# An adaLN block in one kernel: a new share-out of the first norm between ScalarE and VectorE, and a new order of the q phase's columns and of VectorE's list

## The chip, the cores and the metric

The kernel is one launch on one core of one Trainium2 chip. The metric is device time in microseconds; lower is better. The engines go by the names of the profile: PE is TensorE, DVE is VectorE, ACT is ScalarE, POOL is GpSimd, and SP is SyncE, whose queue issues nearly all DMAs.

## The reference, cut to what matters

```python
mod = (silu(c) @ w_mod)                       # 6 vectors of 1024: sa, ca, ga, sb, cb, gb
h = layernorm(x) * (1 + ca) + sa              # x is [2048, 1024], bfloat16
x = x + ga * linear_attention(h, wqkv, wo)    # phi(q), phi(k); phi(t) = t + 1 if t > 0 else exp(t)
h = layernorm(x) * (1 + cb) + sb
x = x + gb * ((silu(h @ w_gate) * (h @ w_up)) @ w_down)
```

Only the first line of h and the q and k products of the attention are touched by the change in earnest. The mean and the variance of the first norm are those of each row of x; the modulation vectors ca and sa come out of a product of the small vector silu(c) with w_mod.

## The kernel before

**Tiles and stages.** The 2048 rows are 16 tiles of 128 rows, in four chunks of four tiles. XRES holds the rows. HT holds, in two buffers (chunk number modulo 2), a chunk's normalised rows turned round: eight slices (dt 0 to 7) of 128 features by 512 rows. The order of the program is: first norm of chunk 0; q phase of chunk 0; k phase of chunk 0; then for each of chunks 1 to 3 eight k groups and eight q groups; then the products that form the attention's output, and the feed-forward part. A group is eight matmuls of 512 columns into one PSUM bank.

**What sets the order.** Every engine runs its own list strictly in the order in which the program text issues it. A helper class records each operation, finds which earlier operations it depends on by the memory it touches (for PSUM by whole banks), and puts in semaphore waits. All operations are recorded through one helper, so every row of the profile has the line L176, and rows are told apart by their tiles. Side work is hung on the groups: `qside`, `kside`, `s1`, `s2`, `s3` are lists of closures that are issued after the group of that number.

**First norm of chunk 0.** The four tiles land at 3.62, 4.24, 5.80 and 6.58 us. Statistics are made in one of two ways: on VectorE (`ln1_stats_ops`: two half-tile bn_stats and an aggregate) or on ScalarE (`act_stats`: one Identity pass and one Square pass with accumulated sums, whose bulk output goes to a junk tile; `act_var` on VectorE then makes the negated variance). In the kernel before, ScalarE sums tile 1 and VectorE does tiles 0, 2 and 3; ScalarE normalises tiles 0 and 1 and VectorE tiles 2 and 3. GpSimd raises the variance to the power -0.5. TensorE turns each tile with eight transposes into PSUM (`tile_transposes`), and fills its waits with matmuls on zeros (`warm`). `mod_sc` makes columns of the modulation on TensorE (one-column matmuls into bank 0), `fin_ca` and `fin_sa` read them out on VectorE. `h0_first` scales a turned slice out of PSUM into HT, `raw_copy` copies two slices without scaling.

**q phase of chunk 0** (`q_phase_chunk0`). The first seven column groups of q go slice by slice, so that the work can begin before all weights and all modulation columns are there; `q_part` is one step of one group. In between stand the `mod_sc` columns, and `bias_mm`, which carries the shift sa through the q weights to a bias column (`BIASQ`), so that the first use of HT needs the scale alone. The eighth group comes last, into bank 0. `h0_shift` then adds the shift to HT for the k phase. `q_phi` evaluates phi: ScalarE writes exp and relu of the bank into four rotating buffers E1 and RL (`phi_evac`), and after each second group VectorE combines them (`phi_flush`). The norm of chunk 1's tiles (4 to 7) is woven into this list, and `th_dma` turns each of these tiles with an x-bar DMA transpose on SP's queue into the other buffer of HT.

**k phase of chunk 0 and chunk 1.** A k group's exp goes to E1 as well, and VectorE's flush reads the PSUM bank itself and so releases it. After the second k group `kside` holds `th_mod(1, dt)`, the eight modulations of chunk 1's slices; after the fourth and fifth it holds ScalarE's passes over tiles 10 and 11. Eight banks rotate; a k group of chunk 1 needs the bank of the k group of the same number of chunk 0.

```python
def th_mod(ch, dt):
    buf = ch % 2
    if dt % 2 == 0 or ch == 1:
        P.dve("tensor_scalar", out=HT[:, buf, dt, :], ...
    else:
        P.act("activation", out=HT[:, buf, dt, :], ...

for dt in range(NDT):
    add(kside, 1, lambda dt=dt: th_mod(1, dt))
for jj, k in ((0, 3), (1, 4)):
    add(kside, k, lambda jj=jj: act_stats(10 + jj))
```

Of the kernel before, what the change touches and what calls it, by code (L numbers as in the profile page):

```python
# [8 lines left out]
ACT = mybir.ActivationFunctionType  # L9
# [253 lines left out]
def bass_adaLN_cond__linear_attn_block__swiglu_ffn__prompt_kernel(  # L263
# [17 lines left out]
    NDT = D // 128  # L281
# [4 lines left out]
    with ExitStack() as es:  # L286
# [114 lines left out]
        def ca_load(p):  # L401
            P.dma("wca%d" % p, WCA[:, :, 512 * p:512 * p + 512], wmv[:, :, D + 512 * p:D + 512 * p + 512])

        def sa_load(p):
            P.dma("wsa%d" % p, WSA[:, :, 512 * p:512 * p + 512], wmv[:, :, 512 * p:512 * p + 512])

        def wq_load(i, n=1):
            P.dma("wq%d" % i, WQK[:, i:i + n, 0:D], wqkvv[:, i:i + n, 0:D])
# [6 lines left out]
        sa_load(1)  # L415
        wq_load(6)
        wq_load(7)
        sa_load(0)
        for j in range(2):
            P.dma("x1_%d" % j, XRES[:, 4 + j, :], xv[:, 4 + j, :])  # L420
        for i in (1, 0):
# [70 lines left out]

        def th_mod(ch, dt):
            buf = ch % 2
            if dt % 2 == 0 or ch == 1:
                P.dve("tensor_scalar", out=HT[:, buf, dt, :], in0=HT[:, buf, dt, :], scalar1=MODCOL[:, 0, dt:dt + 1],
                      scalar2=MODCOL[:, 1, dt:dt + 1], op0=ALU.mult, op1=ALU.add)
            else:
                P.act("activation", out=HT[:, buf, dt, :], in_=HT[:, buf, dt, :], func=ACT.Identity,
                      scale=MODCOL[:, 0, dt:dt + 1], bias=MODCOL[:, 1, dt:dt + 1])  # L500

        mod_first = [True]

        def mod_sc(w, c0, ms):
            for m in ms:
                for kt in range(NDT):
                    P.pe("matmul", out=PS[:, 0, c0 + m:c0 + m + 1], lhsT=w[:, kt, m * 128:(m + 1) * 128],
                         rhs=SILUC[:, kt:kt + 1], start=mod_first[0], stop=(kt == NDT - 1), skip_group_check=True)
                    mod_first[0] = False
# [61 lines left out]

        JUNK1 = T("junk1", 204 * KB, [128, 2, 512], BF16)

        def act_stats(st, c0=0, mid=None):
            n = (D - c0) // 512
            junk0 = HT[:, 1, 0:2, :] if st < 8 else JUNK1
            for fn_, sc_, acc_ in ((ACT.Identity, 1.0 / D, SUMX), (ACT.Square, D ** -0.5, SUMSQ)):
                P.act("activation", out=junk0[:, 0:n, :], in_=XRES[:, st, c0:D].rearrange("p (a b) -> p a b", a=n),
                      func=fn_, scale=sc_, accum_out=acc_[:, st:st + 1])
                if mid is not None:  # L580
                    mid()
                    mid = None

        def act_mv_ops(st):
            return [
# [7 lines left out]
                  op1=ALU.add)  # L593
            P.pool("tensor_tensor", out=RSTD[:, st:st + 1], in0=VE[:, st:st + 1], in1=NEGHALF[:, 0:1], op=ALU.pow)

        s0_, s2_, s3_ = ln1_stats_ops(0), ln1_stats_ops(2), ln1_stats_ops(3)

        def act_var(st):
            P.dve("scalar_tensor_tensor", out=MV[:, st, 1:2], in0=SUMX[:, st:st + 1], scalar=SUMX[:, st:st + 1],
                  in1=SUMSQ[:, st:st + 1], op0=ALU.mult, op1=ALU.subtract)  # L600
            P.dve("tensor_scalar", out=VE[:, st:st + 1], in0=MV[:, st, 1:2], scalar1=-1.0, scalar2=EPS, op0=ALU.mult,
                  op1=ALU.add)

        def act_xn(st, mean):
            P.dve("tensor_scalar", out=NMR[:, st:st + 1], in0=mean, scalar1=RSTD[:, st:st + 1],
                  scalar2=-1.0, op0=ALU.mult, op1=ALU.mult)
            P.act("activation", out=XRES[:, st, :], in_=XRES[:, st, :],
                  func=ACT.Identity, scale=RSTD[:, st:st + 1], bias=NMR[:, st:st + 1])

        def tile_transposes(*js):  # L610
            for dt in range(NDT):
                for j in js:
                    c = (dt % 2) * 512 + j * 128
                    P.pe("transpose", out=PSB[:, 4 + dt // 2, c:c + 128], in_=XRES[:, j, dt * 128:(dt + 1) * 128],
                         identity=IDENT[:])

        warm(13, bank=3)
        act_stats(1)
        for f in s0_:
            f()  # L620
        ln1_rstd1(0)
        s2_[0]()
        s2_[1]()
        act_xn(0, MV[:, 0, 0:1])
        tile_transposes(0)
        warm(5, bank=3)
        act_var(1)
        P.pool("tensor_tensor", out=RSTD[:, 1:2], in0=VE[:, 1:2], in1=NEGHALF[:, 0:1], op=ALU.pow)
        P.pool("tensor_scalar", out=NMR[:, 1:2], in0=SUMX[:, 1:2], scalar1=RSTD[:, 1:2], scalar2=-1.0,
               op0=ALU.mult, op1=ALU.mult)  # L630
        P.act("activation", out=XRES[:, 1, :], in_=XRES[:, 1, :], func=ACT.Identity, scale=RSTD[:, 1:2],
              bias=NMR[:, 1:2])
        s2_[2]()
        ln1_rstd1(2)
        s3_[0]()
        s3_[1]()
        s3_[2]()
        ln1_rstd1(3)
        ln1_xn(2)
        mod_sc(WCA, 8, range(2))  # L640
        tile_transposes(1, 2)
        ln1_xn(3)
        fin_ca(0, 2)
        tile_transposes(3)
        mod_sc(WCA, 8, range(2, 4))
        h0_first(0, "dve")
        h0_first(1, "dve")
        raw_copy(4, "dve")
        raw_copy(6, "act")
# [94 lines left out]

        def q_phase_chunk0(side):
            qb = [1, 2, 3, 4, 6, 7, 5]
            fin_ca(2, 2)
            for dt in (2, 3):
                h0_first(dt, "dve")
            for nts, dts in ((range(4), (0,)), (range(4), (1,)), ((4, 5, 6), (0, 1))):  # L750
                for nt in nts:
                    q_part(nt, qb[nt], dts)
            for nt in range(7):
                if nt == 3:
                    mod_sc(WCA, 8, range(4, 8))
                    fin_ca(4, 4)
                    for dt in (4, 5):
                        h0_scale_only(dt)
                q_part(nt, qb[nt], (2, 3))
            act_stats(4)  # L760
            for nt in range(7):
                if nt == 4:
                    mod_sc(WSA, 0, range(6, 8))
                    fin_sa(6, 2)
                    for dt in (6, 7):
                        h0_scale(dt)
                q_part(nt, qb[nt], (4, 5))
            mod_sc(WSA, 0, range(4, 6))
            fin_sa(4, 2, True)
            for nt in range(7):  # L770
                if nt == 2:
                    bias_mm((4, 5))
                q_part(nt, qb[nt], (6,))
            for nt in range(7):
                if nt == 1:
                    mod_sc(WSA, 0, range(4))
                    fin_sa(0, 4, True)
                    ln_ops[1][0]()
                    ln_ops[1][1]()
                if nt == 4:  # L780
                    bias_mm(range(4))
                    bias_fin()
                q_part(nt, qb[nt], (7,))
            ln_ops[1][2]()
            ln1_rstd1(5)
            for f in act_mv_ops(4):
                f()
            neg_rstd(4)
            q_phi = lambda nt: phi_evac(qb[nt] if nt < 7 else 0, PQT[:, nt, 0:512], bias=BIASQ[:, nt:nt + 1])
            for i, dt in enumerate((4, 5, 0, 1, 2, 3, 6, 7)):  # L790
                P.pe("matmul", out=PS[:, 0, :], lhsT=WQK[:, dt, 896:1024], rhs=HT[:, 0, dt, :], start=(i == 0),
                     stop=(i == 7))
            for dt in (4, 5):
                h0_shift(dt)
            ln1_xn(5)
            th_dma(5)
            for dt in range(4):
                h0_shift(dt)
            ln1_xn(4)
            th_dma(4)  # L800
            for nt in range(8):
                q_phi(nt)
                for f in side.get(nt, []):
                    f()
            qk_ctr[0] = 0

        def add(d, k, f):
            d.setdefault(k, []).append(f)
# [1 line left out]
        qside, kside = {}, {}  # L810
        ln_ops = [ln1_stats_ops(4 + jj) for jj in range(4)]

        def ln_x1(jj):
            for f in ln_ops[jj]:
                f()
            ln1_rstd1(4 + jj)
        for f in ln_ops[2]:
            add(qside, 1, f)
        for f in ln_ops[3]:
            add(qside, 1, f)  # L820
        add(qside, 1, lambda: ln1_rstd2(6))
        for jj in range(2, 4):
            add(qside, 3, lambda jj=jj: ln1_xn(4 + jj))
            add(qside, 3, lambda jj=jj: th_dma(4 + jj))
        for dt in range(NDT):
            add(kside, 1, lambda dt=dt: th_mod(1, dt))
        for jj, k in ((0, 3), (1, 4)):
# [252 lines left out]
        for st in range(NST):  # L1080
            for (sw, nh) in (((0, 0), (1, 0)), ((0, 1), (1, 1)))[st] if st < 2 else ((st, 0), (st, 1)):
                wo_part(sw, nh, range(4, 8) if st < 2 else range(8))
                done = wo_res(sw, nh)
            if st < 4:
                P.wait_for("sp", [done])
                if st < 3:
                    ch = st + 1
                    P.dma("xr%d" % (3 + ch), XRES[:, 4 * ch:4 * ch + 4, :], xv[:, 4 * ch:4 * ch + 4, :])
                else:
                    P.dma("stgx2", STGX[1][:], wmv[:, :, 5120:6144])  # L1090
            if st >= 1:
                ln2_sq(st - 1)
            for kt in ((), (0,), (1,), (2, 3), (4,), (5,), (6, 7))[st] if st < 7 else ():
                macc(STGX[0], kt)
            if st == 6:
                macc_split()
            if st == 8:
                mod_red()
                mod_fin_col(3, False)
            if st == 7:  # L1100
                for jj in range(4):
                    ln2_xn(jj)
                th2_dma()
            if st == 8:
                th2_mod()
            if st == 7:
                for q in range(4):
                    gu_load(q)
# [106 lines left out]
```

## Time and profile before

| What | Value |
|---|---|
| median of the timed runs | 829.2 us (3 runs, 828.35 to 829.22) |
| span of the profiled execution, first to last instruction | 827.0 us |
| PE busy | 817.0 us |
| DVE busy, of these in 30 to 40 us | 310.8 us, 9.90 of 10 |
| ACT busy, of these in 30 to 40 us | 197.3 us, 9.11 of 10 |
| first scaled q matmul on record | 12.71 us |
| landing of the columns 512 to 1023 of sa | 21.36 us |

The profile is that of one execution. The page gives no time of that execution beyond its span; the timed runs lie 1.35 to 2.2 us above it. A row of a timeline has the start and the length in us, the engine, the line (always L176 here), the operation, what it writes and reads, the count, and in brackets the idle time before it and what ended it. Some matmul records are missing, one in about fifty: a step between two matmuls that is exactly twice the usual one is a lost record and no wait.

### The profile page before, as it was taken

To read this page: it belongs to the slowest core of one execution; us is meant where nothing else is said; L and a number is where in the kernel's file an instruction comes from. 1 tells how busy PE (TensorE), PEld (TensorE's weight loads), DVE (VectorE), ACT (ScalarE), POOL (GpSimd) and SP (SyncE) were. 2 spreads that over 40 slices of the span, in tenths; PEclk is the share of its full clock that TensorE was granted. 3 is DMA by queue.
4 is the path that set the end of the run, shared out by engine and by line. 5 is a ranking of instruction groups with operands and counts; after the bars stand their busy time and mean duration, and the time that the engine had idled before them with its cause. 6 is when DMAs were issued, how large, how long until landed. Compare 5 with 4: busy or idle time off the path is not lost.

```text
span 827.0 us, 10428 instructions
## 1 busy us (share of the span) xinstructions
PE 817.0 (99%) x4244; PEld 376.1 (45%) x4323; DVE 310.8 (38%) x664; ACT 197.3 (24%) x336; POOL 40.7 (5%) x59
## 2 busy tenths in 40 slices
PE   8999999999999999999999999999999999999998
PEld 4544444444444444444444444444444444444444
DVE  5798988476945521111221112122111211221111
ACT  4658643123241111011111101111110111111011
POOL 1010000000130000030000003000000300000000
PEclk9999999999999999999999999999999999999999
DMA  9969665856697995700455570045557004553000
GB/s 317 283 151 225 156 169 144 185 166 200 164 256 234 289 256 153 175 27 23 133 149 152 154 177 29 20 128 153 152 153 185 26 19 124 153 153 87 0 26 26
DMA packets 199360, 119.32 MB, mean 144 GB/s; under 512 B 57992, under 2 KB 183056, under 8 KB 199312
## 3 DMA queue, kind: packets, MB, share of 16 engines
q1 hardware_dynamic: 199296, 118.65, 53.7%
q8 instruction: 34, 0.56, 0.3%
q14 instruction: 14, 0.11, 0.0%
q10 hardware_dynamic: 16, 0.00, 0.0%
HBM read 100.67 MB, written 4.33 MB: 127 GB/s over the span
## 4 chain that ended last, share of the span: by engine, by line
PE 95%; DMA 2%; DVE 1%; SPq 1%; issue 1%; ACT 0%; DVEq 0%; ACTq 0%
PE ps L176 95%; DMA wsa<-in_w_mod_dram 2%; DVE acc L176 1%; SPq L176 1%; DVE pkt L176 0%; DVE e L176 0%; DVE pqt L176 0%; ACT e L176 0%; DVE xres L176 0%; DVE ht L176 0%; DVEq L247 0%; ACTq L247 0%
## 5 line engine op out<-in xcount | busy, mean ns | idle before, releaser
L176 PE MATMUL ps<-h2t,gug 128*128 128x512 bf16 x878 | 210.1, 379 | 0.9
L176 PE MATMUL ps<-h2t,guu 128*128 128x512 bf16 x878 | 209.9, 379 | 0.9
L176 DVE TENSOR_TENSOR at<-sg,ps 128x512 bf16<-128x512 bf16 x112 | 77.0, 688 | 282.7 <-PE ps L176 270.5
L176 ACT ACTIVATE sg<-ps 128x512 bf16<-128x512 f32 x112 | 66.9, 597 | 309.7 <-PE ps L176 298.3
L176 PEld LDWEIGHTS ps<-h2t,guu 128*128 128x128 bf16 x896 | 87.7, 98 | 105.7
L176 PEld LDWEIGHTS ps<-h2t,gug 128*128 128x128 bf16 x896 | 87.6, 98 | 105.5
L176 PE MATMUL ps<-wd_a,at 128*128 128x512 bf16 (+1 forms) x502 | 111.9, 377 | 0.5
L176 PE MATMUL ps<-ht,wqk 128*128 128x512 bf16 x499 | 110.5, 379 | 1.0 <-issue 0.2
L176 PE MATMUL ps<-wd_b,at 128*128 128x512 bf16 (+1 forms) x377 | 84.7, 377 | 0.4
L176 PEld LDWEIGHTS ps<-wd_a,at 128*128 128x128 bf16 x512 | 50.1, 98 | 59.7
L176 DVE TENSOR_TENSOR ut<-att,gb_b 128x512 bf16<-128x512 bf16 (+1 forms) x32 | 13.9, 435 | 167.2 <-ACT att L176 167.2
L176 PEld LDWEIGHTS ps<-ht,wqk 128*128 128x128 bf16 x512 | 49.4, 98 | 59.0 <-DVE ht L176 0.7
L176 ACT ACTIVATE att<-ps 128x512 bf16<-128x512 f32 (+1 forms) x32 | 17.4, 591 | 182.1 <-PE ps L176 182.1
L176 PEld LDWEIGHTS ps<-wd_b,at 128*128 128x128 bf16 x384 | 37.5, 98 | 44.7
L176 PE MATMUL ps<-pk,xres 128*128 128x512 bf16 x250 | 55.4, 379 | 0.6 <-issue 0.5
L176 PE MATMUL ps<-mw,pqt 128*128 128x512 bf16 x249 | 55.5, 379 | 0.5 <-issue 0.2
L176 POOL TENSOR_SCALAR h2t<-h2t,modcol 128x512 bf16<-128x512 bf16 x32 | 26.3, 837 | 383.4 <-DMA h2t<-xn 383.4
L176 ACT ACTIVATE e<-ps 128x512 bf16<-128x512 f32 x56 | 33.2, 604 | 31.9 <-PE ps L176 20.2
L176 PEld LDWEIGHTS ps<-mw,pqt 128*128 128x128 bf16 x256 | 24.7, 98 | 30.2 <-issue 0.5
L176 PEld LDWEIGHTS ps<-pk,xres 128*128 128x128 bf16 x256 | 24.7, 98 | 29.9 <-issue 0.9
L176 ACT ACTIVATE junk<-xres 128x1024 bf16<-128x1024 bf16 x24 | 25.4, 1058 | 34.5 <-DVE xres L176 34.2
L176 DVE SCALAR_TENSOR_TENSOR xres<-ps,xres 128x512 bf16<-128x512 f32 x32 | 21.4, 688 | 11.8 <-PE ps L176 11.6
(107 smaller groups left out, 337.9 us busy)
## 6 DMA issues: line engine op xcount, KB each, us to landing
gug<-in_B_w_gate_dram SPq DMA_DIRECT2D x56, 512.0 KB, 4.0
guu<-in_B_w_up_dram SPq DMA_DIRECT2D x56, 512.0 KB, 5.3
xres<-in_A_x_dram SPq DMA_DIRECT2D x20, 256.0 KB, 4.4
rb<-recip_den SPq DMA_DIRECT2D x8, 512.0 KB, 11.5
stgx<-in_w_mod_dram SPq DMA_DIRECT2D x2, 2048.0 KB, 9.7
wd_a<-in_B_w_down_dram SPq DMA_DIRECT2D x4, 1024.0 KB, 7.4
out_dram<-xres SPq DMA_DIRECT2D x31, 128.0 KB, 1.7
xres<-in_A_x_dram SPq DMA_DIRECT2D x3, 1024.0 KB, 7.1
```

The costliest lines, as they stand in the source:

```text
L176: return getattr(e, method)(**kw)
```

## The change

The change has these parts.

- First norm: ScalarE sums tiles 0 and 2, VectorE makes the statistics of tiles 1 and 3. Tile 1 is normalised on VectorE and turned first, then tile 0 (normalised on ScalarE, behind the sums of tile 2), tile 3 and tile 2 (both normalised on VectorE). Five filler matmuls become three. The first four columns of ca are made as one and three, not as two and two; the second `fin_ca` moves from the q phase to a place between `h0_first(0)` and `h0_first(1)`.
- The load of the columns 0 to 511 of sa is split into two halves over kt. The q phase makes the four columns of sa in two parts, one for each half. Other column groups and the two bias products are moved by one to two q steps.
- ScalarE's Identity pass over tile 4 stays in the q phase; its Square pass moves behind `q_phi(1)`. Its junk output goes to JUNK1.
- VectorE's list from the end of the q phase: shifts of slices 4 and 5 first, then the second half of tile 5's statistics, then shifts of 0 to 3, then tile 5. Tile 6's statistics go behind `q_phi(0)`; tile 4's variance, tile 7's statistics, and tile 4's normalising with its transpose go behind `q_phi(1)`; tiles 6 and 7 are normalised and turned behind `q_phi(2)` and no longer behind `q_phi(3)`.
- For chunk 1 `th_mod` puts slices 0, 1 and 2 on ScalarE and 3 to 7 on VectorE.
- In the second norm, `mod_red`, `mod_fin_col(3, False)` and `th2_mod` move from st 8 to st 9.

```diff
-        def sa_load(p):
-            P.dma("wsa%d" % p, WSA[:, :, 512 * p:512 * p + 512], wmv[:, :, 512 * p:512 * p + 512])
+        def sa_load(p, k0=0, k1=8):
+            P.dma("wsa%d_%d" % (p, k0), WSA[:, k0:k1, 512 * p:512 * p + 512], wmv[:, k0:k1, 512 * p:512 * p + 512])
...
-            if dt % 2 == 0 or ch == 1:
+            if dt % 2 == 0 if ch != 1 else dt > 2:
...
         warm(13, bank=3)
-        act_stats(1)
-        for f in s0_:
+        act_stats(0)
+        for f in s1_:
             f()
-        ln1_rstd1(0)
-        s2_[0]()
-        s2_[1]()
-        act_xn(0, MV[:, 0, 0:1])
-        tile_transposes(0)
-        warm(5, bank=3)
-        act_var(1)
...
+        ln1_rstd1(1)
+        act_var(0)
+        pool_pow(0)
+        P.pool("tensor_scalar", out=NMR[:, 0:1], in0=SUMX[:, 0:1], scalar1=RSTD[:, 0:1], scalar2=-1.0,
                op0=ALU.mult, op1=ALU.mult)
...
+        act_stats(2)
         s3_[0]()
+        ln1_xn(1)
         s3_[1]()
         s3_[2]()
         ln1_rstd1(3)
-        ln1_xn(2)
-        mod_sc(WCA, 8, range(2))
-        tile_transposes(1, 2)
+        P.act("activation", out=XRES[:, 0, :], in_=XRES[:, 0, :], func=ACT.Identity, scale=RSTD[:, 0:1],
+              bias=NMR[:, 0:1])
+        act_var(2)
+        pool_pow(2)
+        tile_transposes(1)
+        warm(3, bank=3)
         ln1_xn(3)
-        fin_ca(0, 2)
+        tile_transposes(0)
+        mod_sc(WCA, 8, range(1))
         tile_transposes(3)
-        mod_sc(WCA, 8, range(2, 4))
+        ln1_xn_sum(2)
+        fin_ca(0, 1)
+        tile_transposes(2)
+        mod_sc(WCA, 8, range(1, 4))
         h0_first(0, "dve")
+        fin_ca(1, 3)
         h0_first(1, "dve")
...
             for nt in range(7):
-                if nt == 3:
+                if nt == 4:
                     mod_sc(WCA, 8, range(4, 8))
...
-            act_stats(4)
+            act_stats(4, (0,))
             for nt in range(7):
-                if nt == 4:
+                if nt == 6:
                     mod_sc(WSA, 0, range(6, 8))
...
-                if nt == 2:
+                if nt == 3:
                     bias_mm((4, 5))
...
                 if nt == 1:
-                    mod_sc(WSA, 0, range(4))
+                    mod_sc(WSA, 0, range(4), range(4))
+                if nt == 4:
+                    mod_sc(WSA, 0, range(4), range(4, 8))
                     fin_sa(0, 4, True)
                     ln_ops[1][0]()
-                    ln_ops[1][1]()
-                if nt == 4:
+                if nt == 6:
                     bias_mm(range(4))
                     bias_fin()
                 q_part(nt, qb[nt], (7,))
-            ln_ops[1][2]()
-            ln1_rstd1(5)
-            for f in act_mv_ops(4):
-                f()
-            neg_rstd(4)
...
             for dt in (4, 5):
                 h0_shift(dt)
+            ln_ops[1][1]()
+            ln_ops[1][2]()
+            ln1_rstd1(5)
+            for dt in range(4):
+                h0_shift(dt)
             ln1_xn(5)
             th_dma(5)
-            for dt in range(4):
-                h0_shift(dt)
-            ln1_xn(4)
-            th_dma(4)
...
         for f in ln_ops[2]:
-            add(qside, 1, f)
+            add(qside, 0, f)
+        add(qside, 1, lambda: act_stats(4, (1,)))
+        add(qside, 1, lambda: act_var(4))
+        add(qside, 1, lambda: pool_pow(4))
         for f in ln_ops[3]:
             add(qside, 1, f)
         add(qside, 1, lambda: ln1_rstd2(6))
+        add(qside, 1, lambda: ln1_xn_sum(4))
+        add(qside, 1, lambda: th_dma(4))
         for jj in range(2, 4):
-            add(qside, 3, lambda jj=jj: ln1_xn(4 + jj))
-            add(qside, 3, lambda jj=jj: th_dma(4 + jj))
+            add(qside, 2, lambda jj=jj: ln1_xn(4 + jj))
+            add(qside, 2, lambda jj=jj: th_dma(4 + jj))
...
-            if st == 8:
+            if st == 9:
                 mod_red()
                 mod_fin_col(3, False)
```

`pool_pow(st)` is the power on GpSimd as a helper of its own, and `ln1_xn_sum(st)` normalises a tile on VectorE with ScalarE's sum as the mean.

More of the change, by code (lines that the diff above doesn't have):

```diff
@@ L417, in bass_adaLN_cond__linear_attn_block__swiglu_ffn__prompt_kernel @@
         wq_load(7)
-        sa_load(0)
+        sa_load(0, 0, 4)
+        sa_load(0, 4, 8)
         for j in range(2):
@@ L502, in bass_adaLN_cond__linear_attn_block__swiglu_ffn__prompt_kernel, with mod_sc @@
         mod_first = [True]
-        def mod_sc(w, c0, ms):
+        def mod_sc(w, c0, ms, kts=range(NDT)):
             for m in ms:
-                for kt in range(NDT):
+                for kt in kts:
                     P.pe("matmul", out=PS[:, 0, c0 + m:c0 + m + 1], lhsT=w[:, kt, m * 128:(m + 1) * 128],
@@ L572, in bass_adaLN_cond__linear_attn_block__swiglu_ffn__prompt_kernel, with act_stats @@
         JUNK1 = T("junk1", 204 * KB, [128, 2, 512], BF16)
[L574 to L578, printed above, removed]
+        def act_stats(st, passes=(0, 1)):
+            junk0 = HT[:, 1, 0:2, :] if st < 4 else JUNK1[:]
+            for i in passes:
+                fn_, sc_, acc_ = ((ACT.Identity, 1.0 / D, SUMX), (ACT.Square, D ** -0.5, SUMSQ))[i]
+                P.act("activation", out=junk0, in_=XRES[:, st, :].rearrange("p (a b) -> p a b", a=2),
                       func=fn_, scale=sc_, accum_out=acc_[:, st:st + 1])
-                if mid is not None:
-                    mid()
-                    mid = None
         def act_mv_ops(st):
@@ L594, in neg_rstd @@
             P.pool("tensor_tensor", out=RSTD[:, st:st + 1], in0=VE[:, st:st + 1], in1=NEGHALF[:, 0:1], op=ALU.pow)
-        s0_, s2_, s3_ = ln1_stats_ops(0), ln1_stats_ops(2), ln1_stats_ops(3)
+        s1_, s3_ = ln1_stats_ops(1), ln1_stats_ops(3)
         def act_var(st):
@@ L602, in act_var @@
                   op1=ALU.add)
[L604 to L608, printed above, removed]
         def tile_transposes(*js):
@@ L615, in tile_transposes, with ln1_xn_sum, pool_pow @@
                          identity=IDENT[:])
+        def ln1_xn_sum(st):
+            P.dve("tensor_scalar", out=XRES[:, st, :], in0=XRES[:, st, :],
+                  scalar1=SUMX[:, st:st + 1], scalar2=RSTD[:, st:st + 1], op0=ALU.subtract, op1=ALU.mult)
+        def pool_pow(st):
+            P.pool("tensor_tensor", out=RSTD[:, st:st + 1], in0=VE[:, st:st + 1], in1=NEGHALF[:, 0:1], op=ALU.pow)
         warm(13, bank=3)
-        act_stats(1)
-        for f in s0_:
-            f()
-        ln1_rstd1(0)
-        s2_[0]()
-        s2_[1]()
-        act_xn(0, MV[:, 0, 0:1])
-        tile_transposes(0)
-        warm(5, bank=3)
-        act_var(1)
-        P.pool("tensor_tensor", out=RSTD[:, 1:2], in0=VE[:, 1:2], in1=NEGHALF[:, 0:1], op=ALU.pow)
-        P.pool("tensor_scalar", out=NMR[:, 1:2], in0=SUMX[:, 1:2], scalar1=RSTD[:, 1:2], scalar2=-1.0,
+        act_stats(0)
+        for f in s1_:
+            f()
+        ln1_rstd1(1)
+        act_var(0)
+        pool_pow(0)
+        P.pool("tensor_scalar", out=NMR[:, 0:1], in0=SUMX[:, 0:1], scalar1=RSTD[:, 0:1], scalar2=-1.0,
                op0=ALU.mult, op1=ALU.mult)
[L631 to L634, printed above, removed]
+        act_stats(2)
         s3_[0]()
+        ln1_xn(1)
         s3_[1]()
@@ L746, in q_phase_chunk0 @@
             qb = [1, 2, 3, 4, 6, 7, 5]
-            fin_ca(2, 2)
             for dt in (2, 3):
@@ L811, in bass_adaLN_cond__linear_attn_block__swiglu_ffn__prompt_kernel @@
         ln_ops = [ln1_stats_ops(4 + jj) for jj in range(4)]
[L813 to L816, printed above, removed]
         for f in ln_ops[2]:
-            add(qside, 1, f)
+            add(qside, 0, f)
+        add(qside, 1, lambda: act_stats(4, (1,)))
+        add(qside, 1, lambda: act_var(4))
+        add(qside, 1, lambda: pool_pow(4))
         for f in ln_ops[3]:
@@ L1103, in bass_adaLN_cond__linear_attn_block__swiglu_ffn__prompt_kernel @@
                 th2_dma()
-            if st == 8:
+            if st == 9:
                 th2_mod()
```

## The prediction

> **What bounds the kernel.** I read the page first.
>
> ```profile
> PE 817.0 (99%) x4244; PEld 376.1 (45%) x4323; DVE 310.8 (38%) x664; ACT 197.3 (24%) x336; POOL 40.7 (5%) x59
> ```
>
> TensorE is busy 817.0 of 827.0 us, so a change pays only where TensorE idles or does filler, and any new wait of TensorE goes straight to the end. The next view is TensorE's timeline of the first 45 us (start, length).
>
> ```profile
> 2.61 5.73 PE L176 MATMUL ps<-e,ident 128*128 128x512 bf16 x13 [0.24 <-DVE e L176]
> 8.64 0.62 PE L176 MATMUL ps<-ident,xres 128*128 128x128 bf16 x8 [0.31 <-ACT xres L176]
> 9.10 1.24 PE L176 MATMUL ps<-e,ident 128*128 128x512 bf16 x5
> ...
> 21.41 0.55 PE L176 MATMUL ps<-siluc,wsa 128*128 128x1 bf16 x16 [0.18 <-DMA wsa<-in_w_mod_dram]
> ...
> 28.04 17.21 PE L176 MATMUL ps<-ht,wqk 128*128 128x512 bf16 x77
> ```
>
> Filler (13 and 5 warm matmuls) fills the wait for the first norm. Useful matmuls of 512 columns follow each other by 0.216 us, turns (128 columns) by 0.056, column products by 0.025. From 28.04 on there is one unbroken row: 77 matmuls with 0.1 us of wait. So before 28 us less than 1.5 us can be won. After it there is only something to lose, and what could lose it stands in VectorE's timeline (27 to 47 us), then in ScalarE's (35 to 62 us):
>
> ```profile
> 36.80 0.99 DVE L176 TENSOR_SCALAR xres<-xres,mv,rstd 128x1024 bf16<-128x1024 bf16 x2
> ...
> 43.10 2.67 DVE L176 TENSOR_SCALAR ht<-ht,modcol 128x512 bf16<-128x512 bf16 x8 [1.54 <-DMA ht<-xres]
> ```
>
> ```profile
> 36.58 0.69 ACT L176 ACTIVATE e<-ps,biasq 128x512 bf16<-128x512 f32 x1 [0.89 <-DVE pqt L176]
> ...
> 38.87 2.07 ACT L176 ACTIVATE e<-ps 128x512 bf16<-128x512 f32 x4
> ...
> 59.33 1.21 ACT L176 ACTIVATE e<-ps 128x512 bf16<-128x512 f32 x2 [3.77 <-DVE pkt L176]
> ```
>
> Chunk 1's modulation (eight on VectorE, 0.324 apart) starts as the last x-bar transpose lands (42.98) and ends at 45.78; TensorE needs the last slice at 45.74. While VectorE waits 1.54 us, ScalarE goes on: four exps, then the sums of tiles 10 and 11.
>
> **First norm.** ScalarE gains two passes (2.33 us a tile, 4.27 to 6.60) and loses one normalising (1.24); VectorE loses a tile's statistics (1.29 + 0.21) and gains one normalising (0.54); GpSimd keeps four powers and a shift. By these rows: tile 1 lands 4.24, statistics to 5.98 (1.72 as for tile 0 now), power to 6.70, normalised 7.75. Tile 0 is summed 3.65 to 5.98, but on ScalarE tile 2's sums (6.01 to 8.34) stand ahead of its normalising: 9.55, against 8.59 now. Tile 3: power 9.48, normalised 10.06 (now 10.91). Tile 2: power queued behind tile 3's; the row where a power lay beside a normalising is 0.78 against 0.56, so 10.2, normalised 10.80. TensorE: filler to 8.13, tile 1's turns to 8.58, three fillers to 9.23, wait, tile 0's turns 9.6 to 10.05, eight columns, tile 3's to 10.7, tile 2's 10.86 to 11.3, 24 columns to 11.9. The first scaling out of PSUM ends 11.73, but the second waits for fin_ca(1, 3) behind those columns: 12.33 to 12.81. So q's second slice starts at 12.95, now 13.36: **0.4 won**.
>
> **Columns up to 28 us.** Same matmuls and columns. Gone: the wait for wsa (0.34 with a lost record taken out) because two more matmul pairs stand ahead, and 0.12 of small waits. New: 0.10 for slice 6, 0.07 and 0.23 around the bias, whose copy had three matmuls (0.65) as cover and now one (0.22). Splitting the wsa load adds one issue (0.43) on SP, hidden behind an x issue that sat 4.58 us on a full ring. The eighth group starts at 28.18, now 28.69: **0.5 won**, 0.45 left after a small wait for the shifts.
>
> **VectorE's list, 28 to 38 us.** It now runs without idle time. New: it waits 0.5 us until TensorE has read slice 4 (28.56) before it may shift it, and 0.4 us for the power of tiles 6 and 7 (0.70, row at 35.87). Added up by rows: shifts 0.53, tile 5's second half 1.02, shifts 1.05, normalising 0.46, tile 6 1.43, flush of phi 0/1 1.07, tile 4's variance 0.32, tile 7 1.62, normalising 0.46, then tiles 6 and 7: 38.0, now 37.8. The flush of 2/3 has slipped behind that, and with four buffers ScalarE's exp 6 waits for it: 38.8 instead of 36.58. The exps of k groups 0 and 1 come at 41.1 and 41.6 (now 38.87, 39.35).
>
> **SP.** Tile 4's transpose was issued at 32.9; its input is now ready at 36.7, so three transposes of 1.33 us queue: 36.7, 38.05, 39.4. From issue to landing the transposes at 56 to 64 us took 3.3, this one now 4.3: landing 42.7 or 43.7. Ends: 41.9 (ScalarE is not free before 42.0, however early they land) and 43.8. I take 43.0, nearer the 3.3, since the ring is emptier.
>
> **Chunk 1.** ScalarE takes slices 0 to 2, and everything behind them on its queue waits for the landing too. The view of the tile ht (count, then ns: least, median, most) has the price of one slice on each engine:
>
> ```profile
> L176 DVE TENSOR_SCALAR ht<-ht,modcol x16: 401/406/414, 43.1 to 97.8; 128x512 bf16<-128x512 bf16 x16
> ...
> L176 ACT ACTIVATE ht<-ht,modcol x8: 804/814/827, 65.1 to 97.4; 128x512 bf16<-128x512 bf16 x8
> ```
>
> ScalarE's take 0.81, 0.705 apart (70.66 to 71.36). Start 43.12, third slice 45.34, where TensorE, 0.45 early, wants it at 44.2: **+1.08**. Behind them: exps of k groups 2 to 7 and four passes. Exp 2 starts 45.24, exp 3 45.71; from there to exp 5's end the row is 6.04 (40.30 to 46.34): 51.7. VectorE frees the bank 0.9 later, 52.6; k group 4 of chunk 1 wants it at 51.87: **+0.79**. VectorE then begins tile 8's statistics at 54.8 instead of 50.57; from there 8.7 to the release of bank 3 (59.28): 63.4, wanted at 63.0: **+0.45**. ScalarE's next exp waits for the same (the 3.77 above), 63.45 for 59.33, and from there to 76 it has no slack (15.58 busy in 59.3 to 75.4), so chunk 2's last slice, 72.18 now, comes at 76.3. Chunk 2 starts 73.83 and wants it at 75.34: **+1.02**. Afterwards ScalarE waits 1.13 of every 1.73 us for TensorE and VectorE 1.07 at 83.2: the lag is gone, and the loss stays. The move of mod_red by one tile takes away a 0.06 wait at 227; the last use of H2T's modulation (POOL, done 234.6, then 3 later) is at 244, so that is hidden.
>
> Sum: -0.45 + 1.08 + 0.79 + 0.45 + 1.02 = **+2.9**, on a span of 827.0; the timed runs (median 829.2) lie 2.2 above the span, which I leave: 832.1.
>
> **Two rules weighed.** Modulation on ScalarE costs 0.705 a slice by the rows above, on VectorE 0.324. The Trainium skill, Perfetto Trace Analysis, Optimizing Scalar/DVE Operations, says moving work to ScalarE may pay when VectorE is saturated. By it VectorE's list would shorten by three slices, 0.97, and the sum for that step would be a gain instead of +1.08; I go by the rows, as VectorE sits idle just before and ScalarE's queue does not.
>
> The fillers follow each other by 0.427 until 8.1 and later matmuls by 0.216. The skill's TensorE: Matmul & The Clock Gate, Part 1, has the clock at half rate until a free-running window of about 3.4 us was busy. Tile 1's turns come 0.5 us earlier than any turn now; by it they and three fillers could be at half rate, 1.0 more, of which 0.37 lies in the wait for tile 0. No row here shows a turn at half rate; the first one, 0.3 us after the fillers, ran at 0.056, and the sum goes by that.
>
> **Rivals.** (1) The chain as summed: the price moves one for one with ScalarE's start, start - 40.2; with starts of 42.0 to 43.9, +1.9 to +3.7. Chance 0.60. (2) Only the first two waits count, as banks and buffers downstream have more slack than I read: -0.45 + 1.08 + 0.8, or less: +0.6 to +1.5. For it: each later wait is a small difference of long sums. 0.17. (3) Not slower: VectorE's list and the transposes get through early, ScalarE starts slices 0 to 2 by 40.2, and no wait is new; the 0.5 from the front stays: 828.7. It decides at 40.2. For it: the stalls of packets at 34.1 to 36.8 and 40.0 to 41.5 may go. Against: three issues of 1.33 from 36.7. 0.11. (4) Worse: a transpose stalls again (1.5 us at 40.0 to 41.5) and the new turns run at 0.107: +4 to +5. 0.10. What I have not seen: 0.02.
>
> Range 829.6 to 833.9: it leaves out (3), the end of (4) and the unseen, some 0.16. A difference of 0.2% (1.66 us) is about what measuring can tell from none. Faster by more: 0.02, the unseen. Within: (2) and (3), 0.28. Slower: (1) and (4), 0.70.
>
> **What would show it.** q's second slice at 12.9; the eighth group at 28.2; tile 7's normalising ending at 38.0; last transpose landing near 43; three ScalarE modulations 0.705 apart with idle time of ScalarE before them; TensorE waits at 44 to 46, 52, 63 and 74 to 76. Wrong if ScalarE starts them by 40, or if TensorE's row from 44 to 76 stays unbroken.

## The result and the profile after

The changed kernel takes 831.64 us (median of 5 runs, 831.08 to 832.9), the kernel before on the same chip 828.7 (5 runs, 828.27 to 829.22): ratio 1.004, 95% interval 1.0029 to 1.0051, so 2.9 us slower. The profiled span is 829.8 against 827.0. One execution of an experiment, e1's profiled one, took 1238.73 us where the other ten of that kernel took 829.23 to 830.91; it counts in nothing below.

Of the page, the row of busy times and the chain, by engine, come first.

```profile
PE 817.5 (99%) x4242; PEld 375.7 (45%) x4321; DVE 309.3 (37%) x658; ACT 200.2 (24%) x342; POOL 41.2 (5%) x59
...
PE 94%; DVE 3%; ACT 1%; issue 1%; DMA 1%; POOL 0%; ACTq 0%
```

TensorE has as much to do as before (817.0 then, 817.5 now), so nearly all of the 2.8 us of span are waits. TensorE's timeline shows them. Up to 30 us (start, length, count, wait and releaser in brackets):

```profile
8.37 0.61 PE L176 MATMUL ps<-ident,xres 128*128 128x128 bf16 x8
8.81 0.81 PE L176 MATMUL ps<-e,ident 128*128 128x512 bf16 x3
9.47 0.62 PE L176 MATMUL ps<-ident,xres 128*128 128x128 bf16 x8
...
12.69 4.27 PE L176 MATMUL ps<-ht,wqk 128*128 128x512 bf16 x19 [0.17 <-DVE ht L176]
...
27.70 2.51 PE L176 MATMUL ps<-ht,wqk 128*128 128x512 bf16 x10
```

The last row holds the bias wait (0.18 before the matmul at 28.10, with which the eighth group starts). From 30 us on:

```profile
29.84 14.75 PE L176 MATMUL ps<-ht,wqk 128*128 128x512 bf16 x64
44.90 6.65 PE L176 MATMUL ps<-ht,wqk 128*128 128x512 bf16 x30 [0.32 <-ACT ht L176]
52.20 10.53 PE L176 MATMUL ps<-ht,wqk 128*128 128x512 bf16 x47 [0.65 <-DVE pkt L176]
63.07 11.61 PE L176 MATMUL ps<-ht,wqk 128*128 128x512 bf16 x52 [0.34 <-DVE pkt L176]
75.26 4.97 PE L176 MATMUL ps<-ht,wqk 128*128 128x512 bf16 x20 [0.58 <-ACT ht L176]
```

The one row of before (unbroken from 28.04 to 80.3) is cut in five. The bracket counts idle time after the last modelled end; the loss is the step between two starts less the usual 0.216: 0.27 (at 44.20, inside the first row) + 0.49 at 44.90, 0.81 at 52.20, 0.50 at 63.07, 0.74 + 0.26 at 75.26 and 75.96. ScalarE's timeline has the cause (27 to 78 us):

```profile
38.92 0.69 ACT L176 ACTIVATE e<-ps,biasq 128x512 bf16<-128x512 f32 x1 [2.66 <-DVE pqt L176]
...
41.22 1.10 ACT L176 ACTIVATE e<-ps 128x512 bf16<-128x512 f32 x2
42.62 2.22 ACT L176 ACTIVATE ht<-ht,modcol 128x512 bf16<-128x512 bf16 x3 [0.30 <-DMA ht<-xres]
44.75 1.05 ACT L176 ACTIVATE e<-ps 128x512 bf16<-128x512 f32 x2
...
63.05 1.21 ACT L176 ACTIVATE e<-ps 128x512 bf16<-128x512 f32 x2 [5.02 <-DVE pkt L176]
```

ScalarE takes its three slices as the transpose lands, 0.705 apart, and the exps behind them, at 39.82 before, come at 44.75. Of these 4.93 us, 2.35 are there already at the first exp of the k phase (41.22 for 38.87, as VectorE's new list keeps exp 6 waiting), 0.45 come at the landing and 2.13 are the three slices. VectorE (27 to 56 us) hands the delay on:

```profile
37.15 1.00 DVE L176 TENSOR_SCALAR xres<-xres,mv,rstd 128x1024 bf16<-128x1024 bf16 x2 [0.60 <-POOL rstd L176]
...
43.78 1.70 DVE L176 TENSOR_SCALAR ht<-ht,modcol 128x512 bf16<-128x512 bf16 x5
...
51.24 0.29 DVE L176 TENSOR_SCALAR e<-e 128x512 bf16<-128x512 bf16 x1 [2.41 <-ACT e L176]
```

It waits 2.41 us for an exp of ScalarE before it may release the bank that TensorE wants at 52.

### The profile page after: what moved, and what is told of

Same layout as the page of the kernel before. It is cut to its first block, busy times and chain, and to the rows that moved or that the text cites. A ratio compares the mean times of both kernels' runs of the same rounds, so it can differ in the third digit from the quotient of the medians.

```text
span 829.8 us, 10427 instructions
## 1 busy us (share of the span) xinstructions
PE 817.5 (99%) x4242; PEld 375.7 (45%) x4321; DVE 309.3 (37%) x658; ACT 200.2 (24%) x342; POOL 41.2 (5%) x59
## 4 chain that ended last, share of the span: by engine, by line
PE 94%; DVE 3%; ACT 1%; issue 1%; DMA 1%; POOL 0%; ACTq 0%
PE ps L176 94%; DVE pkt L176 1%; DVE stats L176 1%; ACT ht L176 0%; DVE xres L176 0%; DMA ht<-xres 0%; DVE ht L176 0%; ACT junk L176 0%; DVE e L176 0%; ACT rl L176 0%; DMA cs<-in_c_dram 0%; ACT e L176 0%; POOL rstd L176 0%; DVE mv L176 0%; DVE pqt L176 0%
## 5 line engine op out<-in xcount | busy, mean ns | idle before, releaser
L176 ACT ACTIVATE junk<-xres 128x1024 bf16<-128x1024 bf16 x26 | 27.5, 1056 | 46.1 <-DVE xres L176 34.2
```

What stands on the lines that cost most here:

```text
L176: return getattr(e, method)(**kw)
```

## The experiments

**Which part costs?** Theory: ScalarE's share of chunk 1's slices. Rivals: VectorE's list, or all of it together. Three kernels follow; the kernel before, run beside them, took 828.78.

e1, all eight slices back on VectorE, the rest as changed:

```diff
-            if dt % 2 == 0 if ch != 1 else dt > 2:
+            if dt % 2 == 0 or ch == 1:
```

> The changed kernel, with all eight slices of chunk 1's modulation back on VectorE; all else stays changed. My theory (ScalarE's three slices block the exps and sums queued behind them): VectorE starts the eight at 43.78, when its flush is done, so slice 7 is ready at 46.5 and chunk 1's first k group ends at 46.7 (46.06 in the kernel before); ScalarE does exps and tile 10's sums meanwhile, and the waits of TensorE near 52, 63 and 75 us vanish. Time: +0.7 on the kernel before, 829.4. The rival (VectorE's new list and the late transposes are the cause, whoever modulates): the waits near 52, 63 and 75 stay, +2 or more, 830.7 to 831.6.

830.06 us, ratio 1.0017 (1.0008 to 1.0026): between the two, so taking the split back returns 1.6 of the 2.9, and something else costs as well. A trace of this kernel is shown with e8, below.

e2, the kernel before with the same line changed the other way (slices 0 to 2 on ScalarE, nothing else):

> The kernel before with one edit: slices 0 to 2 of chunk 1's modulation go to ScalarE. My theory: ScalarE waits from 39.9 for the landing at 42.98, the third slice is ready at 45.3, chunk 1's first k group ends at 46.7, then TensorE waits near 52 (0.8), 63 (0.4) and 75 (1.0): +2.9 to +3.0, 831.7, as much as the whole change. The rival (the list's order is the cause): 828.7 to 829.3, with a wait at 44 to 46 alone.

831.62 us, ratio 1.0035 (1.0021 to 1.0049), as expected: one line makes the whole loss. Its trace, ScalarE and then TensorE:

```profile
38.68 1.10 ACT L176 ACTIVATE e<-ps 128x512 bf16<-128x512 f32 x2
42.81 2.23 ACT L176 ACTIVATE ht<-ht,modcol 128x512 bf16<-128x512 bf16 x3 [3.04 <-DMA ht<-xres]
...
63.24 1.21 ACT L176 ACTIVATE e<-ps 128x512 bf16<-128x512 f32 x2 [5.02 <-DVE pkt L176]
```

```profile
45.09 6.65 PE L176 MATMUL ps<-ht,wqk 128*128 128x512 bf16 x30 [0.32 <-ACT ht L176]
52.39 10.53 PE L176 MATMUL ps<-ht,wqk 128*128 128x512 bf16 x47 [0.65 <-DVE pkt L176]
63.27 11.61 PE L176 MATMUL ps<-ht,wqk 128*128 128x512 bf16 x52 [0.34 <-DVE pkt L176]
75.45 4.76 PE L176 MATMUL ps<-ht,wqk 128*128 128x512 bf16 x19 [0.57 <-ACT ht L176]
```

Here the price is bare: with the old list ScalarE stands idle for 3.04 us ahead of the slices, with work queued behind them. TensorE's waits at the same four places (0.14 + 0.49, 0.81, 0.50, 0.74 + 0.26) are those of the changed kernel, but for 0.13 in the first. The exps behind the slices come at 44.94, 5.12 later than before. The span is 2.7 above that of before.

e3, the new front and the new order of the q columns, with the old list and all slices on VectorE (two pieces of the edit; its other lines put the list and the second norm back as in the kernel before):

```diff
-            act_stats(4, (0,))
+            act_stats(4)
...
-            if dt % 2 == 0 if ch != 1 else dt > 2:
+            if dt % 2 == 0 or ch == 1:
```

> The new first norm and the new places of the q phase's columns alone; VectorE's list for chunk 1, the modulation and the second norm as in the kernel before. My theory: the eighth q group begins 0.5 us earlier (28.2 for 28.7), but chunk 1's first k group still ends at 46.06, as its slices wait for the transposes (landing near 43.0) and eight modulations: TensorE waits about 0.6 at 44 to 46, and the time is that of the kernel before, 828.7 (within 0.1). A rival that the gain in front reaches the end: 828.2. A rival that the front itself costs (turns at half clock): 829.0 or more, and the eighth group later than 28.7.

829.23 us, ratio 1.0006 (0.9997 to 1.0015): no gain, and perhaps a little loss. TensorE and VectorE in its trace:

```profile
10.49 0.35 PE L176 MATMUL ps<-siluc,wca 128*128 128x1 bf16 x8 [0.40 <-DMA wca<-in_w_mod_dram]
```

```profile
43.88 2.67 DVE L176 TENSOR_SCALAR ht<-ht,modcol 128x512 bf16<-128x512 bf16 x8 [1.56 <-DMA ht<-xres]
```

In this execution the front won little: the first half of ca's columns landed at 10.45 (9.79 before), the eighth group started at 28.59 (28.69 before), and after two small waits (0.2 in all) TensorE came to chunk 1 at 44.35, no earlier than before (44.2). The transposes landed 0.77 later than before (43.75 for 42.98), the slices came 0.324 apart, and TensorE, which takes one in 0.216, waited 7 x 0.107 = 0.75. So the trace shows the price of a later landing; that an earlier TensorE would wait for the same landing is argued and not shown by it. The expected rival, turns at half rate, is there too: the first four turns, from 8.14, are 0.107 apart, the rest 0.056. It cost nothing here, as tile 0's turns start at 9.47, as in the changed kernel.

**What is the list worth?** e4 is the kernel before with the new list of VectorE, the new q-side order and ScalarE's two passes over tile 4 apart; front, columns and slices as before. Its edit is that part of the diff above, from `act_stats(4, (0,))` to `th_dma(4 + jj)`, less the columns and the slices.

> Theory (the late ScalarE start costs most, the new list of VectorE a smaller part through the later landing): the front stays as before, so k group 0 of chunk 1 wants its slices at 44.2 us; the last transpose lands near 43.5 to 44, all eight slices go on VectorE 0.324 apart from 43.9 to 44.3, slice 7 is ready at 46.6 to 47.0 and the k group ends 0.6 to 1.2 us later than the 46.06 of the kernel before; no wait of TensorE at 52, 63 and 75. Time 829.4 to 830.0. Rival (the list costs nothing, its lateness is hidden like the rest): 828.8, and the first k group of chunk 1 ends at 46.1.

830.18 us against 828.46 for the kernel before beside it, ratio 1.0019 (1.0011 to 1.0028), span 828.5. VectorE and TensorE:

```profile
44.58 2.67 DVE L176 TENSOR_SCALAR ht<-ht,modcol 128x512 bf16<-128x512 bf16 x8 [0.39 <-DMA ht<-xres]
```

```profile
27.78 16.41 PE L176 MATMUL ps<-ht,wqk 128*128 128x512 bf16 x75
45.05 35.24 PE L176 MATMUL ps<-ht,wqk 128*128 128x512 bf16 x159 [0.85 <-DVE ht L176]
```

So the list costs 1.5 (span) to 1.7 (runs) by itself, nearly all in the first k group of chunk 1: 1.02 + 7 x 0.107 = 1.77 of waits, less 0.34 (for wsa) and 0.10 of before that this run hasn't, is 1.3 of the span's 1.5. The row from 45.05 on is unbroken: nothing at 52, 63 or 75. The landing, 44.45, was later than I expected, but VectorE is busy with its own list until 44.19, so it accounts for 0.39 at most.

e8 is e1's kernel once more:

> The changed kernel with all eight slices of chunk 1 on VectorE, once more, for a trace of it. By its timed runs (830.06) it is 1.3 us above the kernel before. Theory: the last transpose lands at 42.5 to 43.0, VectorE comes free at 43.8 and ends slice 7 at 46.5, TensorE waits some 0.7 in the first k group of chunk 1, and 1.0 of front gain is not kept; waits at 52, 63 and 75 are gone. Rival (the later waits come from VectorE's list and not from ScalarE's lateness): the waits of 0.81, 0.50 and 1.0 at 52, 63 and 75 are still there.

830.28 us, ratio 1.0022 (1.0013 to 1.0031), span 828.3. ScalarE and TensorE:

```profile
41.27 2.07 ACT L176 ACTIVATE e<-ps 128x512 bf16<-128x512 f32 x4
```

```profile
44.81 35.45 PE L176 MATMUL ps<-ht,wqk 128*128 128x512 bf16 x160 [0.89 <-DVE ht L176]
```

Again one wait (1.06 + 0.75) and no later ones, so the rival falls: 52, 63 and 75 come from ScalarE's lateness. The list alone makes the exps 2.4 late (41.27 for 38.87), and that is made up without a wait. The wait was 1.8 and not 0.7: the landing was 44.21 and not 42.5 to 43.0, which held VectorE up by 0.43, and the front's lead of 0.55, which the 0.7 left out, turned into a wait too. Less this lead the 1.8 is the +1.3 of the span.

**Is it the place in ScalarE's queue?** e6 is the changed kernel with ScalarE's sums of tile 10 ahead of the k phase, so that they aren't behind the slices:

```diff
-        for jj, k in ((0, 3), (1, 4)):
-            add(kside, k, lambda jj=jj: act_stats(10 + jj))
+        add(qside, 5, lambda: act_stats(10))
+        add(kside, 4, lambda: act_stats(11))
```

> The changed kernel, with the sums of tile 10 (two ScalarE passes, 2.36 us) moved from behind k group 3 into the q phase behind the sixth phi, where ScalarE stood idle for 2.66 us; the slices stay on ScalarE. My theory: what stands behind the three slices is 2.36 shorter, so exp 5 ends at 48.9 for 51.2: the waits at 52 and 63 vanish, that near 75 shrinks to 0.5, and those at 44 to 46 stay. Time +0.6 on the kernel before, 829.3. If the queue behind the slices is not the price, the time stays at 831.6.

829.9 us (829.03 to 832.65), ratio 1.0017 (1.0008 to 1.0026), 0.6 over the expected time. TensorE in the profiled run, one of the longer ones (831.52):

```profile
46.11 0.38 PE L176 MATMUL ps<-ht,wqk 128*128 128x512 bf16 x1 [1.41 <-ACT ht L176]
46.73 0.39 PE L176 MATMUL ps<-ht,wqk 128*128 128x512 bf16 x1 [0.24 <-ACT ht L176]
47.43 32.90 PE L176 MATMUL ps<-ht,wqk 128*128 128x512 bf16 x148 [0.31 <-ACT ht L176]
```

ScalarE starts its slices 2.5 us later than in the changed kernel (45.15, with 2.01 of idle time before, as the last transpose landed at 45.05). TensorE pays at once, 2.5 in all, and then nothing at 52 and 63, and 0.12 at 76. As TensorE and ScalarE are now both 2.5 later, the first exps behind the slices are as late for TensorE as in the changed kernel; but 2.3 us less is queued behind them, and the later exps are in time. Here a wait of an engine costs by what stands behind it.

e7 is the kernel before with slices 3 and 6 on ScalarE, but behind the sums of tile 10:

```diff
-            if dt % 2 == 0 or ch == 1:
+            if dt % 2 == 0 if ch != 1 else dt not in (3, 6):
...
-        for dt in range(NDT):
+        for dt in (0, 1, 2, 4, 5, 7):
             add(kside, 1, lambda dt=dt: th_mod(1, dt))
-        for jj, k in ((0, 3), (1, 4)):
-            add(kside, k, lambda jj=jj: act_stats(10 + jj))
+        add(kside, 3, lambda: act_stats(10))
+        for dt in (3, 6):
+            add(kside, 3, lambda dt=dt: th_mod(1, dt))
+        add(kside, 4, lambda: act_stats(11))
```

> The kernel before, with slices 3 and 6 of chunk 1 on ScalarE, but behind its sums of tile 10, where it comes by at 43.1 us, after the landing (42.98). Theory (what costs is the place in ScalarE's queue ahead of the landing, not ScalarE's 0.705 us a slice): no idle time of ScalarE before them; VectorE is through with its six at 45.1 rather than 45.8; the exp behind them comes 1.4 us later and still ahead of its bank's need at 51.9. Time 828.7, within 0.3 either way. Rival (any slice on ScalarE costs TensorE, as it takes twice as long and delays the exps behind): over 829.5, with waits at 52, 63 or 75.

828.89 us against 828.46, ratio 1.0004 (0.9995 to 1.0013): no difference that can be measured. ScalarE and TensorE:

```profile
43.56 1.52 ACT L176 ACTIVATE ht<-ht,modcol 128x512 bf16<-128x512 bf16 x2
```

```profile
28.44 51.74 PE L176 MATMUL ps<-ht,wqk 128*128 128x512 bf16 x239
```

No idle time before the slices, and TensorE's row is whole. (The transposes landed 0.5 later than before, but TensorE was 0.4 later too: its eighth group starts at 29.09.) So two slices of 0.705 behind the landing cost nothing; three there were not tried. What decides is how late the exps behind are: 2.4 (e8, where TensorE itself came 1.3 later) was made up, 4.9 and 5.1 (the changed kernel, e2) were not, and in e2 3.04 of it is idle time ahead of the landing.

**A version that keeps the front's gain?** e5: front as changed, list as before, slices as in e7.

> The changed front and q columns, the list of VectorE as before, and slices 3 and 6 of chunk 1 on ScalarE behind the sums of tile 10. With the front alone the eight slices on VectorE held the first k group of chunk 1 back by 7 x 0.107 us, 0.75, after a landing at 43.75. Theory: with two slices on ScalarE the last slice is ready at 45.9 rather than 46.55, the k group ends 0.6 us earlier than with the front alone, and there are no new waits later: 828.6 (828.2 to 828.9). Rival (the front's gain is lost in the landing, whatever follows): 829.2 as with the front alone.

828.83 us (828.26 to 829.8), ratio 1.0002 (0.9993 to 1.0011).

```profile
27.67 52.57 PE L176 MATMUL ps<-ht,wqk 128*128 128x512 bf16 x241
```

The profiled span is 826.5, 0.5 under that of before, with no wait after 32 us. But the profiled run is the shortest of the 11, and over all of them no gain can be measured. No version here beats the kernel before.

**Why do transposes land now after 3.3, now after 4.9 us?** Four runs on the coincidence told in the last section. e9 and e12 are e1's kernel with idle copies on VectorE and on ScalarE, e10 is the changed kernel and e11 e5's kernel with those on VectorE:

```diff
+            def tiny(n):
+                for _ in range(n):
+                    P.dve("tensor_copy", out=MEAN2[:, 0:4], in_=NEGHALF[:])
...
+            tiny(22)
...
+                    tiny(22)
```

```diff
+            for _ in range(24):
+                P.act("activation", out=MEAN2[:, 0:4], in_=NEGHALF[:], func=ACT.Identity)
             act_stats(4, (0,))
```

> The changed kernel with all eight slices on VectorE, and 44 copies of 128x4 elements added to VectorE where it idles (14 to 17.9 and 18.7 to 22.1 us); nothing reads them. In eight of nine traces a 16 KB packet of the instruction queue starts as VectorE comes by its 92nd to 96th instruction, at 39.5 to 43.0 us, and the transposes in flight then take 4.1 to 5.0 us; only in the changed kernel's own trace it starts at 45.56, behind them, and they take 3.2 to 3.3. Theory (the packet is VectorE's own instructions, and it holds the transposes up): it moves to 25 to 31 us, tile 7's transpose lands 3.3 us after its issue, at 42.6 instead of 44.2, VectorE starts the slices as it comes free, at 43.8 instead of 44.3, and the time is 829.8 against 830.3. Rival (the coincidence means nothing, or the packet is another engine's): packet at 42, landing at 44.2, time 830.3 or more.

> The changed kernel as it is, with the same 44 small copies. Theory: its own times came in two groups (831.1 to 831.6, and 832.9), and the higher one is that of runs in which the packet meets tile 7's transpose, which ScalarE's slices wait for; with the packet moved the landing is 42.5 in every run, and the times lie at 831.0 to 831.7. Rival (the spread has another cause): a median of 831.6 with some runs at 832.9.

> Front as changed, list as before, slices 3 and 6 on ScalarE behind its sums of tile 10, and the same 44 small copies. Theory: tile 7's transpose, issued at 38.9, lands at 42.2 and tile 6's at 40.9; VectorE starts at 42.3 instead of 43.1; TensorE had no wait there in the trace without the copies, so the gain is only in the runs with a late landing: 828.3 (828.0 to 828.6), 0.4 under the 828.8 without them. Rival (the front's small waits of 0.9 and the jitter of the loads decide): 828.8.

> The changed kernel with all eight slices on VectorE, and 24 passes of 128x4 elements added to ScalarE where it idles (13.9 to 25.7 us); nothing reads them. The 44 copies on VectorE didn't move the packet of the instruction queue against the other work (44.21 in a kernel that ran 2.07 later, 42.14 without), so it isn't VectorE's. Theory (it is ScalarE's): with 24 instructions more ahead it comes 8 us or more earlier, before the transposes; tile 7's transpose lands 3.3 us after its issue, at 42.6 instead of 44.2, VectorE starts the slices at 43.8 instead of 44.3, and the time is 829.8 against 830.3. Rival (another engine's, or the landing is late for another reason): the packet at 42.1, landing at 44.2, 830.3.

The theory missed in all four: 831.6, 832.7, 829.71 and 830.37 us (ratios 1.0035, 1.0054, 1.0015, 1.0022); e12 came out at its rival. VectorE's copies were not hidden:

```profile
14.72 4.45 DVE L176 COPY mean<-neghalf 128x4 f32<-128x4 f32 x22
```

They take 0.20 each and hold up the columns of sa (TensorE waits 1.18 at 24.4 in e9); the three lost 0.9 to 1.3 against the same kernels without copies. The packet stayed with the other work (44.21 in e9, 2.07 later than in e8, while VectorE's list ran 2.05 later; 42.62 in e12, 0.48 later, while ScalarE's list ran 0.56 later). If a packet comes at a fixed place of its engine's list, it is neither VectorE's nor ScalarE's; that it does is assumed. e10's later waits are the changed kernel's (0.17 + 0.49, 0.81, 0.50, 0.74 + 0.26), 1.2 us later.

## Why the prediction was right

- **Front**: tile 1's turns 8.37 (8.13 predicted), tile 0's 9.47 (9.6), q's second slice 12.69 (12.95), eighth group 28.10 (28.18). Right within 0.3, but partly by luck: with the same front the eighth group starts at 28.07 to 28.92 in e5, e8, e3, e12 and e6, and with the old one at 28.43 to 29.09 in e4, e2, the kernel before and e7. The means, 28.42 and 28.68, lie 0.3 apart, and the landing of the loads moves either by more.
- **Half rate**: in this trace the new turns ran at 0.056 right behind the fillers, with the next fillers at the full 0.216, as the sum had it. The half rate for which the prediction cited the Trainium skill's TensorE: Matmul & The Clock Gate, Part 1, did show in e3, for four turns (0.107 apart, to 8.54), worth 0.2 and hidden in the wait for tile 0, not 1.0.
- **VectorE's list and SP**: tiles 6 and 7 normalised at 38.15 (38.0), exp 6 at 38.92 (38.8), transposes issued at 36.58, 37.86 and 39.25 (36.7, 38.05, 39.4). Right. The landing was 42.52 and not 43.0; the prediction chose between 3.3 and 4.3 from issue to landing, and this run had 3.27. The runs with 4.9 lie outside both. So the landing was luck too: in e8, which runs the same operations up to there, it was 44.21. A ScalarE that starts then would by the prediction's rule have cost some 4.0 (an estimate); the two longer runs of the changed kernel, 832.85 and 832.9, would fit that, but no run shows that it is their cause.
- **Chunk 1**: ScalarE from 42.62 (43.12). First k group 0.76 for 1.08, bank 0.81 for 0.79, next release 0.50 for 0.45, chunk 2 1.00 for 1.02. Four of four waits in the place and the size foreseen; only the first was mis-sized, mainly by the landing.
- **Sum**: at chunk 2 the loss is 3.07 - 0.59 (front) - 0.10 (a wait of before that is gone) = 2.4, as the prediction's own rule gives for a start at 42.62 (start - 40.2; by it the low end of the starts, 42.0, is +1.8 and not +1.9). Most of the rest of 2.8 is 0.36 at 176.73 (0.20 of it bracketed "issue"), which before hasn't and the prediction neither. So +2.9 came out partly because errors of 0.5 and 0.4 cancel.
- **What the prediction didn't see**: it derives ScalarE's late start from the list (exp 6 late, ScalarE not free before 42.0). That is true of this kernel (it waits only 0.30 for the landing) but isn't needed: with the old list ScalarE waits 3.04, the start is 42.81, and the loss the same. And the list has a price of its own, 1.7, that hides behind the split's: the parts alone add up to 2.8 + 1.7 + 0.4 = 5.0, together they cost 2.9. The list's lateness of ScalarE takes the place of the wait, and ScalarE takes three of the slices that the list makes late on VectorE, so that the first k group waits 0.76 and not e8's 1.81.
- **Rival (3)**, that 0.5 from the front would stay, is refuted twice: the start was not by 40.2, and the front alone brought no gain that can be measured (e3).
- **The rule weighed**: the Trainium skill, Perfetto Trace Analysis, Optimizing Scalar/DVE Operations, says that moving work to ScalarE may make sense when VectorE is saturated. Here it didn't: three slices moved cost 1.1 to 1.7 us with the new list (the changed kernel against e8 and e1, each less the kernel before beside it) and 2.8 with the old; two moved behind the landing cost and won nothing.

## What to carry to other kernels

An engine that works through its list in order should not be given an operation that waits for a transfer while urgent work stands behind it: ask first where in the list the engine will be when the data land, put the operation there, and add up how late the work behind it gets. A share-out that evens busy times says nothing of this. And before making a bound engine arrive earlier, check that its next input can come earlier too: in the two traces with the new front and the old list (e5, e3) the last transpose landed at 42.95 and 43.75, against 42.98 before.

## What the runs showed of the hardware that was not expected

**Transposes and a packet of instructions.** A 16 KB packet of the instruction queue (q8, 0.9 us long) falls near chunk 1's last transposes in every trace. The DMA view, 37.2 to 44 us, of the kernel before, then of e8, then of the changed kernel (queue: packets, MB, share; of an issue the last number is the median time to landing):

```profile
q8 instruction: 1, 0.02, 0.8%
...
ht<-xres SPq DMA_TRANSPOSE x2, 4.6
```

```profile
q8 instruction: 1, 0.02, 0.8%
...
ht<-xres SPq DMA_TRANSPOSE x3, 3.4
```

```profile
q1 hardware_dynamic: 3463, 1.34, 84.4%
...
ht<-xres SPq DMA_TRANSPOSE x3, 3.3
```

The changed kernel has q1 alone in that window. Where the packet starts while transposes are in flight (11 of 13 traces), the last one takes 4.0 to 5.0 us from issue to landing (4.34 before, 4.92 in e8, whose median hides it, 4.97 in e6). In the two traces where it starts after the landing (45.56 in the changed kernel, 46.45 in e10) all three take 3.2 to 3.3. That is a coincidence in thirteen traces, not a cause shown: the packet could not be moved by itself, and which engine's instructions it holds stays open. e8 and the changed kernel run the same operations up to 42 us, so why the packet came 3.4 later in one is open too. The packet may be why the times of the changed kernel and of e6 spread over 1.8 and 3.6 us.

**Small instructions** of 4 elements cost 0.20 us each in a chain on VectorE and 0.235 on ScalarE (24 in 5.63).

**When TensorE reaches its full rate** differs between executions. The fillers start 0.427 apart and end 0.216 apart where the change falls among them: at about 5.4 us in e4, 6.6 in e9. In e3 it falls among the turns, at 8.5. In the kernel before all fillers (the last starts at 7.70) are at the slower step, and the turns, from 8.64, at the faster.
